# An S5 state-space block with a gated unit on one core: one full-row phase of TensorE per chunk, and a last output tile in parts of 192 and 256 columns

## The chip, the core and the metric

The kernel runs on one core of a Trainium2 chip. The metric is the device time of one execution in microseconds (us); lower is better. A profile comes with each run. Its span runs from the first to the last instruction of the core and is as a rule some 1.8 us shorter than the time measured from outside. All timed runs quoted here are fast ones (TensorE clock granted at 0.988 to 1.0), except one of a variant and two single runs, which are marked.

## The reference

2048 tokens of width D = 448 are normalised. One branch is a complex diagonal recurrence with 448 states and a skip term; the other is a gated unit with F = 1792. The output combines them.

```python
def reference(x, Lambda_re, Lambda_im, B_re, B_im, C_re, C_im, log_dt, Dskip, w_gate, w_up, w_down):
    xn = layernorm(x)                                   # (2048, 448)
    # --- state-space branch
    Lam_bar = exp(exp(log_dt) * Lam)                    # complex, 448 states
    B_bar = ((Lam_bar - 1) / Lam)[:, None] * B
    Bu = xn @ B_bar.T                                   # complex
    h[t] = Lam_bar * h[t - 1] + Bu[t]                   # 2048 steps
    s = 2 * real(h @ C.T) + xn * Dskip                  # xn * Dskip is the skip term
    # --- gated branch
    g = silu((sigmoid(xn @ w_gate) * (xn @ w_up)) @ w_down)
    return x + s * g                                    # bf16
```

## The kernel before

The tokens are worked on in 4 chunks of 512 (4 tiles of 128 each). TensorE has these kinds of work, and how many rows of its array they use matters here:

- **gate and up products**: 14 per chunk, each of seven 64-row *pairs* (two matmuls of 512 columns at once on the two halves of the array). Each goes to one of three PSUM buffers `gu`. A gate product is emptied by ScalarE (tanh), an up product by VectorE, which multiplies it with the tanh.
- **B projection**: the input of the recurrence, in four column groups. 448 = 3 x 128 + 64 input rows, so each group has full-row matmuls ("fulls") and one half-row pair. ScalarE copies the result to `bus` in SBUF.
- **down product** of a tile: 14 full-row matmuls of 448 columns; ScalarE's silu puts it into one of five buffers `g_t`.
- **output tile** (`yout`): 7 full-row matmuls; VectorE adds the skip term `xd`, multiplies by `g_t` and adds x; then a store.

The two PSUM banks `acc` take the down products and the output tiles in turn. The recurrence itself (rotation, scan, rotation back) is VectorE's. A planner places the instructions of ScalarE, VectorE and GpSimd by estimated costs and deadlines; TensorE's order is as written.

```python
def gu_mm(c, k, m, a, lo, hi, first):              # one gate or up product: 7 pairs
    def f():
        for s in range(7):
            T.matmul(gu[a][:, 0, ts], lhsT=w_[0:H, s, ms], rhs=x[0:H, s, ts], start=(s == 0), stop=(s == 6))
            T.matmul(gu[a][:, 1, ts], lhsT=w_[H:P, (s + 1) % 7, ms], rhs=x[H:P, s, ts], ...)
    ...
def gu_evac(c, k, m, a):
    if k == "g": add("ACT", ..., A.activation(th, gu[a][:], ACT.Tanh, scale=0.5), ...)
    else:        add("DVE", ..., V.scalar_tensor_tensor(out=ho, in0=th, scalar=1.0, in1=gu[a][:], op0=ALU.add, op1=ALU.mult), ...)

def b_units(c, pts, mid=None):                     # two column groups of the B projection
    slots = [next_gu() for _ in pts]
    def pairs():
        for pt, a in zip(pts, slots):              # half rows first (start=True)
            ...
    add("PE", 0.216 * len(pts), pairs, ...)
    if mid:
        mid()                                      # down products, in the same full-row stretch
    for n, (pt, a) in enumerate(zip(pts, slots)):
        def fulls(pt=pt, a=a):
            ...                                    # 2 x 3 matmuls, 512 columns (group 3: 256)
        add("PE", ..., fulls, ...)
        if pt < 3:
            add("ACT", act(1024), A.copy(out=bus[u][:], in_=gu[a][:]), ...)
        else:                                      # group 3: one copy of 512 columns, two of 64 rows
            add("ACT", act(512), ...); add("ACT", 0.6, ...); add("ACT", 0.6, ...)

def yout(c, j, first=False, banks=None, parts=((0, D),)):
    for pi, (c0, c1) in enumerate(parts):
        ...
        for i, (hm, cm) in enumerate(K_ORDER):     # 7 matmuls of c1 - c0 columns
            T.matmul(y, lhsT=hT[c % 2][:, hm, js], rhs=cT[:, cm, c0:c1], start=(i == 0), stop=(i == 6))
        V.tensor_tensor(out=od, in0=y, in1=xq[:, c0:c1], op=ALU.add)       # skip term
        V.tensor_tensor(out=od, in0=od, in1=g_t[g][:, c0:c1], op=ALU.mult)
        V.tensor_tensor(out=od, in0=od, in1=x_all[:, t, c0:c1], op=ALU.add)
        ...                                                                # store

# --- order of work (cut)
b_units(0, (0, 1)); b_units(0, (2, 3))             # chunk 0
...
for c in (2, 3):                                   # chunk 1 is alike
    for i in range(0, 4): gu_step(c, i)
    b_units(c, (0, 1), lambda: down(c - 1, 0, True))
    yout(c - 2, 0); down(c - 1, 1); yout(c - 2, 1)
    for i in range(4, 7): gu_step(c, i, i == 4)
    b_units(c, (2, 3), lambda: down(c - 1, 2, True))
    yout(c - 2, 2); down(c - 1, 3); yout(c - 2, 3)
    for i in range(7, 14): gu_step(c, i, i == 7)
    whole(c)                                       # the recurrence of chunk c
...
yout(3, 3, banks=[...], parts=((0, 128), (128, 448)))
```

## Time and profile before

| | before |
|---|---|
| time, median of 3 (range) | 186.65 us (186.59 to 187.62) |
| span of the profiled run | 185.5 us |
| TensorE, VectorE, ScalarE busy | 97%, 89%, 50% |
| matmuls; ScalarE instructions | 1375; 140 |
| switches between half-row and full-row work after 29 us | 17 |

The prediction shows the main lines. Two more, from the page's groups of instructions of the kernel before (line, engine, operation, output from input, shapes, count; busy us and mean ns; idle time before them and what ended most of it):

```profile
L709 PE MATMUL gu<-xnT,wU 64*128 64x512 bf16 x196 | 46.0, 376 | 0.0
...
L726 DVE SCALAR_TENSOR_TENSOR hF<-sig,gu 128x1024 bf16<-128x1024 f32 x21 | 25.4, 1212 | 1.9 <-PE gu L710 1.6
```

A pair shows 376 ns because its end is modelled; pairs start every 0.216 us. VectorE's evacuation of an up product lasts 1.21 us and in 21 of them it waited 1.9 us in all: VectorE rarely has time to wait for TensorE.

One line of the start, from the timeline of VectorE of the kernel before (start, duration, instruction, idle time and releaser in brackets), becomes important later. It is the first use of the x rows of chunk 1, which a transfer of 448 KB brings:

```profile
17.63 0.63 DVE L425 BATCH_NORM_STATS2 bst<-x_all 128x6 f32<-128x448 bf16 x1 [5.26 <-DMA x_all<-in_A_x_dram]
```

VectorE stood idle for 5.26 us until those rows landed, and everything that follows on VectorE starts from there.

### The profile page before, as it was taken

To read this page: it belongs to the slowest core of one execution; us is meant where nothing else is said; L and a number is where in the kernel's file an instruction comes from. 1 tells how busy PE (TensorE), PEld (TensorE's weight loads), DVE (VectorE), ACT (ScalarE), POOL (GpSimd) and SP (SyncE) were. 2 spreads that over 40 slices of the span, in tenths; PEclk is the share of its full clock that TensorE was granted. 3 is DMA by queue.
4 is the path that set the end of the run, shared out by engine and by line. 5 is a ranking of instruction groups with operands and counts; after the bars stand their busy time and mean duration, and the time that the engine had idled before them with its cause. 6 is when DMAs were issued, how large, how long until landed. Compare 5 with 4: busy or idle time off the path is not lost.

```text
span 185.5 us, 3527 instructions
## 1 busy us (share of the span) xinstructions
PE 179.9 (97%) x1375; PEld 88.5 (48%) x1375; DVE 165.8 (89%) x295; ACT 93.1 (50%) x140; POOL 38.5 (21%) x93
## 2 busy tenths in 40 slices
PE   7999999999999999999999999999999999999991
PEld 2675444464445444444445444444445544455550
DVE  3731999999989899999999999899999999999763
ACT  3449995973899994225375422427223516211110
POOL 7125451940168937000012100000000000000000
PEclk9999999999999999999999999999999999999998
DMA  5999999499302330000023300000000000002120
GB/s 159 257 221 225 176 175 210 80 269 178 120 4 46 82 71 4 0 0 4 0 51 78 73 26 0 4 25 24 0 25 4 25 25 4 25 0 76 51 78 25
DMA packets 30257, 13.43 MB, mean 72 GB/s; under 512 B 19744, under 2 KB 30240, under 8 KB 30240
## 3 DMA queue, kind: packets, MB, share of 16 engines
q1 hardware_dynamic: 28336, 12.05, 31.1%
q10 hardware_dynamic: 1808, 1.15, 2.5%
q8 instruction: 11, 0.18, 0.4%
q14 instruction: 6, 0.05, 0.1%
q0 software_dynamic: 96, 0.00, 0.0%
HBM read 6.77 MB, written 1.84 MB: 46 GB/s over the span
## 4 chain that ended last, share of the span: by engine, by line
PE 68%; DVE 15%; DMA 8%; ACT 4%; issue 2%; SPq 1%; DVEq 0%
PE gu L709 29%; PE acc L892 15%; PE acc L917 11%; PE gu L892 6%; DMA x_all<-in_A_x_dram 5%; PE gu L777 5%; DVE hF L726 4%; DMA wG<-in_B_w_gate_dram 3%; DVE wv L831 2%; DVE hT L581 1%; DVE bst L425 1%; ACT ctmp L675 1%; DVE ta L824 1%; PE gu L780 1%; DVE tb L825 1%
## 5 line engine op out<-in xcount | busy, mean ns | idle before, releaser
L709 PE MATMUL gu<-xnT,wG 64*128 64x512 bf16 (+1 forms) x231 | 46.1, 344 | 0.3 <-DVE xnT L510 0.3
L710 PE MATMUL gu<-xnT,wG 64*128 64x512 bf16 (+1 forms) x231 | 46.1, 344 | 0.0
L709 PE MATMUL gu<-xnT,wU 64*128 64x512 bf16 x196 | 46.0, 376 | 0.0
L710 PE MATMUL gu<-xnT,wU 64*128 64x512 bf16 x196 | 46.0, 376 | 0.0
L723 ACT ACTIVATE sig<-gu 128x1024 f32<-128x1024 f32 x21 | 21.4, 1022 | 30.3 <-PE gu L710 27.9
L892 PE MATMUL acc<-wd,hF 128*128 128x448 bf16 x168 | 33.8, 353 | 0.0
L892 PEld LDWEIGHTS <-hF 128*128 128x128 bf16 x224 | 21.4, 98 | 21.1 <-issue 1.7
L709 PEld LDWEIGHTS <-wG 64*128 64x128 bf16 x231 | 21.3, 94 | 20.9 <-issue 1.9
L709 PEld LDWEIGHTS <-wU 64*128 64x128 bf16 x196 | 18.1, 94 | 23.4 <-issue 1.3
L726 DVE SCALAR_TENSOR_TENSOR hF<-sig,gu 128x1024 bf16<-128x1024 f32 x21 | 25.4, 1212 | 1.9 <-PE gu L710 1.6
L831 DVE TENSOR_TENSOR_SCAN wv<-c_r,st,z 128x512 bf16<-128x512 f32 x18 | 22.9, 1275 | 0.0
L917 PE MATMUL acc<-cT,hT 128*128 128x448 bf16 (+1 forms) x112 | 22.4, 344 | 0.0
L710 PEld LDWEIGHTS <-wG 64*128 64x128 bf16 x231 | 21.2, 94 | 0.0
L710 PEld LDWEIGHTS <-wU 64*128 64x128 bf16 x196 | 18.1, 94 | 0.0
L777 PE MATMUL gu<-xnT,bT 128*128 128x512 bf16 x72 | 16.9, 379 | 0.0
L917 PEld LDWEIGHTS <-hT 128*128 128x128 bf16 x119 | 11.3, 98 | 10.0 <-issue 0.4
L898 ACT ACTIVATE g_t<-acc 128x448 bf16<-128x448 f32 x12 | 6.5, 540 | 16.1 <-PE acc L892 13.0
L425 DVE BATCH_NORM_STATS2 bst<-x_all 128x6 f32<-128x448 bf16 x12 | 7.0, 612 | 7.4 <-DMA x_all<-in_A_x_dram 7.4
L788 ACT CAST bus<-gu 128x1024 bf16<-128x1024 f32 x12 | 12.0, 1005 | 2.3 <-PE gu L777 2.3
L478 POOL COPY xn<-xn 128x64 bf16<-128x64 bf16 x12 | 5.9, 488 | 29.1 <-ACT xn L475 28.8
L923 DVE TENSOR_TENSOR o_t<-acc,xd 128x448 bf16<-128x448 f32 (+1 forms) x16 | 9.5, 595 | 2.6 <-PE acc L917 2.4
L898 ACT ACTIVATE g_t<-gu 128x448 bf16<-128x448 f32 x4 | 2.2, 544 | 18.8 <-PE gu L892 18.8
(142 smaller groups left out, 261.8 us busy)
## 6 DMA issues: line engine op xcount, KB each, us to landing
out_dram<-o_t SPq DMA_DIRECT2D x15, 112.0 KB, 1.7
wd<-in_B_w_down_dram SPq DMA_DIRECT2D x2, 784.0 KB, 5.1
x_all<-in_A_x_dram SPq DMA_DIRECT2D x3, 448.0 KB, 4.7
wU<-in_B_w_up_dram SPq DMA_DIRECT2D x2, 448.0 KB, 11.5
wU<-in_B_w_up_dram SPq DMA_DIRECT2D x2, 336.0 KB, 7.3
wG<-in_B_w_gate_dram SPq DMA_DIRECT2D x2, 224.0 KB, 6.1
wG<-in_B_w_gate_dram ACTq DMA_DIRECT2D x2, 224.0 KB, 6.2
xnT<-xn SPq DMA_TRANSPOSE x24, 2.4
```

What stands on the lines that cost most here:

```text
L425: add("DVE", 0.6, lambda: V.bn_stats(out=bst[b][:], in_=x_all[:, t, :]), r=[("x", t)], w=[("bst", b)])
L709: T.matmul(gu[a][:, 0, ts], lhsT=w_[0:H, s, ms], rhs=x[0:H, s, ts], start=(s == 0), stop=(s == 6))
L710: T.matmul(gu[a][:, 1, ts], lhsT=w_[H:P, (s + 1) % 7, ms], rhs=x[H:P, s, ts], start=(s == 0), stop=(s == 6))
L723: add("ACT", act(1024), lambda: A.activation(th, gu[a][:], ACT.Tanh, scale=0.5), r=[("gu", a)], w=[tk])
L726: add("DVE", dve1(1024), lambda: V.scalar_tensor_tensor(out=ho, in0=th, scalar=1.0, in1=gu[a][:], op0=ALU.add, op1=ALU.mult), r=[("gu", a) ...
L777: T.matmul(gu[a][:, i, :], lhsT=bT[:, kt, i, pt * P:pt * P + P], rhs=x[:, 2 * kt, :], start=False, stop=(kt == 2))
L788: add("ACT", act(1024), lambda u=u, a=a: A.copy(out=bus[u][:], in_=gu[a][:]), r=[("gu", a)], w=[("bus", u)])
L831: dve(1.194, lambda k=k: V.tensor_tensor_scan(out=wv[:, k, :], data0=rb, data1=z[:, k, :], initial=(st[pt][:, k, :] if c else 0.0), op0=AL ...
L892: T.matmul(d, lhsT=hF[c % 2][:, m, h, js], rhs=wd[:, ft, :], start=(ft == 0), stop=(ft == FT - 1))
L898: add("ACT", act(448), lambda: A.activation(g_t[g][:], d, ACT.Silu, scale=0.5), r=[key, "silutab"], w=[("gt", g)])
L917: T.matmul(y, lhsT=hT[c % 2][:, hm, js], rhs=cT[:, cm, c0:c1], start=(i == 0), stop=(i == 6))
L923: add("DVE", dve1(n), lambda od=od, y=y, c0=c0, c1=c1: V.tensor_tensor(out=od, in0=y, in1=xq[:, c0:c1], op=ALU.add), r=[key, ("xd", q)], w ...
```

## The change

The intent is to change less often between half-row and full-row work on TensorE, and to shorten VectorE's last instructions after the last matmul. The two `b_units` of a chunk become one `b_phase`: half rows of groups 3, 0 and 1; then their fulls; then all down products and output tiles; then the fulls of group 2, whose half rows come last, so that they join the half-row stream after it. Group 3 moves from a `gu` buffer to the two `acc` banks, with six evacuations of 256 columns. The last tile is cut at column 192, and the skip term of its second part is added by a matmul with the identity.

```diff
-    def b_units(c, pts, mid=None):
+    def b_phase(c, mid=None):
+        slots = [next_gu() for _ in range(3)]
+        a3 = (next_acc(), next_acc())
 ...
+                for h, (d, q, l) in enumerate(((slice(0, P), slice(0, P), 0), (slice(0, H), slice(H, P), 1),
+                                               (slice(H, P), slice(0, H), 1))):
+                    add("ACT", 0.3, lambda ...: A.copy(out=bus[u][d, l, ns], in_=acc[a3[i]][q, 0:256]), ...)
 ...
+        add("PE", 0.54, pairs, ...)                       # half rows of 3, 0, 1
+        for pt in (3, 0, 1):
+            add("PE", ..., lambda pt=pt: fulls(pt, False), ...)
+            evac(pt)
+        if mid:
+            mid()
+        add("PE", 1.29, lambda: fulls(2, True), ...)
+        add("PE", 0.22 + SW, lambda: halfrows(2, False), ...)
+        evac(2)
@@ yout
+            on_pe = len(parts) > 1 and pi == len(parts) - 1
+                if on_pe:
+                    T.matmul(y, lhsT=ident[:, :], rhs=xq[:, c0:c1], start=True, stop=False)
 ...
+            if on_pe:
+                V.tensor_tensor(out=od, in0=y, in1=g_t[g][:, c0:c1], op=ALU.mult)   # no add of xq
@@ order of work
-    b_units(0, (0, 1))
-    b_units(0, (2, 3))
-    for i in range(13, 14):
-        gu_step(0, i, i == 13)
+    gu_step(0, 13)
+    b_phase(0)
 ...
     for c in (2, 3):
+        def mid(c=c):
+            for j in range(4):
+                down(c - 1, j)
+                yout(c - 2, j)
         for i in range(0, 4):
             gu_step(c, i)
-        b_units(c, (0, 1), lambda: down(c - 1, 0, True))
-        ...                                               # yout, down, yout, three gu_steps
-        b_units(c, (2, 3), lambda: down(c - 1, 2, True))
-        ...
-        for i in range(7, 14):
-            gu_step(c, i, i == 7)
+        b_phase(c, mid)
+        for i in range(4, 14):
+            gu_step(c, i)
 ...
-    yout(3, 3, banks=[(("acc", a), acc[a]), free_banks[4]], parts=((0, 128), (128, 448)))
+    yout(3, 3, banks=[(("acc", a), acc[a]), free_banks[4]], parts=((0, 192), (192, 448)))
```

More of the change, by code (lines that the diff above doesn't have):

```diff
@@ L750 @@
     bus_n = [0]
-    def b_units(c, pts, mid=None):
+    def b_phase(c, mid=None):
         x = xnT[c % 3]
-        slots = [next_gu() for _ in pts]
-        bk = [("bT", 0), ("bT", 1), ("bT3", 0), ("bT3", 1), "bT3l"] + (
-            [("bT6", 0), ("bT6", 1)] + [("bT6", i, h) for i in range(2) for h in range(2)] if 3 in pts else [])
-        def pairs():
-            for pt, a in zip(pts, slots):
-                if pt < 3:
-                    ps = slice(pt * P, pt * P + P)
-                    T.matmul(gu[a][:, 0, :], lhsT=bT[0:H, 3, 0, ps], rhs=x[0:H, 6, :], start=True, stop=False)
-                    T.matmul(gu[a][:, 1, :], lhsT=bT[H:P, 3, 1, ps], rhs=x[H:P, 5, :], start=True, stop=False)
-                else:
-                    T.matmul(gu[a][:, 0, 0:256], lhsT=bT6[0:H, 3, :], rhs=x[0:H, 6, 0:256],
-                             start=True, stop=False)
-                    T.matmul(gu[a][:, 1, 0:256], lhsT=bT6[H:P, 3, :], rhs=x[H:P, 5, 256:512],
-                             start=True, stop=False)
-        add("PE", 0.216 * len(pts), pairs, r=xr(c) + bk, w=[("gu", a) for a in slots], name=f"bp{c}.{pts[0]}")
-        if mid:
-            mid()
-        for n, (pt, a) in enumerate(zip(pts, slots)):
-            def fulls(pt=pt, a=a):
-                for i in range(2):
-                    for kt in range(3):
-                        if pt < 3:
-                            T.matmul(gu[a][:, i, :], lhsT=bT[:, kt, i, pt * P:pt * P + P], rhs=x[:, 2 * kt, :],
-                                     start=False, stop=(kt == 2))
-                        else:
-                            T.matmul(gu[a][:, i, 0:256], lhsT=bT6[:, kt, :],
-                                     rhs=x[:, 2 * kt, i * 256:i * 256 + 256], start=False, stop=(kt == 2))
-            add("PE", (6 * 0.215 if pt < 3 else 6 * 0.11) + (0 if n or mid else SW), fulls,
-                r=xr(c) + bk + [("gu", a)], w=[("gu", a)], name=f"b{c}.{pt}")
@@ new lines, in b_phase, with halfrows @@
+        slots = [next_gu() for _ in range(3)]
+        a3 = (next_acc(), next_acc())
+        bk = [("bT", 0), ("bT", 1), ("bT3", 0), ("bT3", 1), "bT3l"]
+        bk6 = [("bT6", 0), ("bT6", 1)] + [("bT6", i, h) for i in range(2) for h in range(2)]
+        rs = [(slice(0, H), 6), (slice(H, P), 5)]
+        def halfrows(pt, start):
+            for i, (hs, s_) in enumerate(rs):
+                if pt < 3:
+                    T.matmul(gu[slots[pt]][:, i, :], lhsT=bT[hs, 3, i, pt * P:pt * P + P], rhs=x[hs, s_, :],
+                             start=start, stop=not start)
+                else:
+                    T.matmul(acc[a3[i]][:, 0:256], lhsT=bT6[hs, 3, :], rhs=x[hs, s_, i * 256:i * 256 + 256],
+                             start=start, stop=not start)
@@ new lines, in pairs, with fulls @@
+        def pairs():
+            for pt in (3, 0, 1):
+                halfrows(pt, True)
+        def fulls(pt, first):
+            for i in range(2):
+                for kt in range(3):
+                    if pt < 3:
+                        T.matmul(gu[slots[pt]][:, i, :], lhsT=bT[:, kt, i, pt * P:pt * P + P], rhs=x[:, 2 * kt, :],
+                                 start=(first and kt == 0), stop=(not first and kt == 2))
+                    else:
+                        T.matmul(acc[a3[i]][:, 0:256], lhsT=bT6[:, kt, :],
+                                 rhs=x[:, 2 * kt, i * 256:i * 256 + 256], start=False, stop=(kt == 2))
@@ L784, in b_units, with key, evac @@
+        def key(pt):
+            return [("gu", slots[pt])] if pt < 3 else [("acc", a) for a in a3]
+        def evac(pt):
             u = bus_n[0] % NBUS
@@ L787, in b_units @@
             if pt < 3:
-                add("ACT", act(1024), lambda u=u, a=a: A.copy(out=bus[u][:], in_=gu[a][:]),
-                    r=[("gu", a)], w=[("bus", u)])
-            else:
-                h2 = lambda t: t.rearrange("p (i n) -> p i n", i=2)
-                add("ACT", act(512), lambda u=u, a=a: A.copy(out=h2(bus[u][:, 0, :]), in_=gu[a][:, :, 0:256]),
-                    r=[("gu", a)], w=[("bus", u)])
-                add("ACT", 0.6, lambda u=u, a=a: A.copy(out=h2(bus[u][0:H, 1, :]), in_=gu[a][H:P, :, 0:256]),
-                    r=[("gu", a)], w=[("bus", u, 1)])
-                add("ACT", 0.6, lambda u=u, a=a: A.copy(out=h2(bus[u][H:P, 1, :]), in_=gu[a][0:H, :, 0:256]),
-                    r=[("gu", a)], w=[("bus", u, 2)])
+                add("ACT", act(1024), lambda: A.copy(out=bus[u][:], in_=gu[slots[pt]][:]), r=key(pt), w=[("bus", u)])
+                return
+            for i in range(2):
+                ns = slice(i * 256, i * 256 + 256)
+                for h, (d, q, l) in enumerate(((slice(0, P), slice(0, P), 0), (slice(0, H), slice(H, P), 1),
+                                               (slice(H, P), slice(0, H), 1))):
+                    add("ACT", 0.3, lambda ns=ns, d=d, q=q, l=l, i=i: A.copy(out=bus[u][d, l, ns], in_=acc[a3[i]][q, 0:256]),
+                        r=[("acc", a3[i])] + ([("bus", u, i, 0)] if h else []),
+                        w=[("bus", u) if h == i == 0 else ("bus", u, i, h)])
+        add("PE", 0.54, pairs, r=xr(c) + bk + bk6, w=key(3) + key(0) + key(1), name=f"bp{c}")
+        for pt in (3, 0, 1):
+            add("PE", (1.29 if pt < 3 else 0.66) + (SW if pt == 3 else 0), lambda pt=pt: fulls(pt, False),
+                r=xr(c) + bk + bk6 + key(pt), w=key(pt), name=f"b{c}.{pt}")
+            evac(pt)
+        if mid:
+            mid()
+        add("PE", 1.29, lambda: fulls(2, True), r=xr(c) + bk, w=key(2), name=f"b{c}.2")
+        add("PE", 0.22 + SW, lambda: halfrows(2, False), r=xr(c) + bk + key(2), w=key(2), name=f"bp{c}.2")
+        evac(2)
     bus_of = {}
@@ L858, in ssm_stack @@
         dve(dve2(1024), lambda: V.tensor_tensor(out=ta[:], in0=bus[u][:], in1=cs3[:], op=ALU.mult),
-            [("bus", u), ("bus", u, 1), ("bus", u, 2)] + tk, [("ta", ia)])
+            [("bus", u)] + [("bus", u, i, h) for i in range(2) for h in range(3) if i or h] + tk, [("ta", ia)])
         dve(dve2(512), lambda: V.tensor_tensor(out=z[:, 0, :], in0=ta[:, 0, :], in1=ta[:, 1, :], op=ALU.add),
@@ L913, in yout, with f @@
             y = y[:, 0:c1 - c0]
-            def f(y=y, c0=c0, c1=c1):
+            on_pe = len(parts) > 1 and pi == len(parts) - 1
+            def f(y=y, c0=c0, c1=c1, on_pe=on_pe):
+                if on_pe:
+                    T.matmul(y, lhsT=ident[:, :], rhs=xq[:, c0:c1], start=True, stop=False)
                 for i, (hm, cm) in enumerate(K_ORDER):
-                    T.matmul(y, lhsT=hT[c % 2][:, hm, js], rhs=cT[:, cm, c0:c1], start=(i == 0), stop=(i == 6))
+                    T.matmul(y, lhsT=hT[c % 2][:, hm, js], rhs=cT[:, cm, c0:c1],
+                             start=(i == 0 and not on_pe), stop=(i == 6))
             n = c1 - c0
-            add("PE", 7 * (0.004 + n / 2400.0) + (SW if first else 0), f,
-                r=cTk + [("hT", c % 2, p) for p in range(4)], w=[key], name=f"y{c}.{j}")
+            add("PE", (8 if on_pe else 7) * (0.004 + n / 2400.0) + (SW if first else 0), f,
+                r=cTk + [("hT", c % 2, p) for p in range(4)] + ([("xd", q), "ident"] if on_pe else []),
+                w=[key], name=f"y{c}.{j}")
             ok = ("o", o, pi)
             od = o_t[o][:, c0:c1]
-            add("DVE", dve1(n), lambda od=od, y=y, c0=c0, c1=c1: V.tensor_tensor(out=od, in0=y, in1=xq[:, c0:c1], op=ALU.add),
-                r=[key, ("xd", q)], w=[ok])
-            add("DVE", dve2(n), lambda od=od, c0=c0, c1=c1: V.tensor_tensor(out=od, in0=od, in1=g_t[g][:, c0:c1], op=ALU.mult),
-                r=[ok, ("gt", g)], w=[ok])
+            if on_pe:
+                add("DVE", dve1(n), lambda od=od, y=y, c0=c0, c1=c1: V.tensor_tensor(out=od, in0=y, in1=g_t[g][:, c0:c1], op=ALU.mult),
+                    r=[key, ("gt", g)], w=[ok])
+            else:
+                add("DVE", dve1(n), lambda od=od, y=y, c0=c0, c1=c1: V.tensor_tensor(out=od, in0=y, in1=xq[:, c0:c1], op=ALU.add),
+                    r=[key, ("xd", q)], w=[ok])
+                add("DVE", dve2(n), lambda od=od, c0=c0, c1=c1: V.tensor_tensor(out=od, in0=od, in1=g_t[g][:, c0:c1], op=ALU.mult),
+                    r=[ok, ("gt", g)], w=[ok])
             add("DVE", dve2(n), lambda od=od, c0=c0, c1=c1: V.tensor_tensor(out=od, in0=od, in1=x_all[:, t, c0:c1], op=ALU.add),
@@ L1005 @@
     prepare(2)
-    b_units(1, (0, 1), lambda: down(0, 0, True))
-    down(0, 1)
-    for i in range(3, 6):
-        gu_step(1, i, i == 3)
-    b_units(1, (2, 3), lambda: down(0, 2, True))
-    down(0, 3)
-    for i in range(6, 14):
-        gu_step(1, i, i == 6)
+    b_phase(1, lambda: [down(0, j) for j in range(4)])
+    for i in range(3, 14):
+        gu_step(1, i)
     whole(1)
     for c in (2, 3):
+        def mid(c=c):
+            for j in range(4):
+                down(c - 1, j)
+                yout(c - 2, j)
         for i in range(0, 4):
             gu_step(c, i)
-        b_units(c, (0, 1), lambda: down(c - 1, 0, True))
-        yout(c - 2, 0)
-        down(c - 1, 1)
-        yout(c - 2, 1)
-        for i in range(4, 7):
-            gu_step(c, i, i == 4)
-        b_units(c, (2, 3), lambda: down(c - 1, 2, True))
-        yout(c - 2, 2)
-        down(c - 1, 3)
-        yout(c - 2, 3)
+        b_phase(c, mid)
         if c == 2:
             prepare(3)
-        for i in range(7, 14):
-            gu_step(c, i, i == 7)
+        for i in range(4, 14):
+            gu_step(c, i)
         whole(c)
```

## The prediction

> **What bounds the kernel now.** I read the busy shares first, then the waits of TensorE, then the chain of work that ended last, then the timelines of TensorE and VectorE. First the busy line of the page, then the whole answer on TensorE's waits (engine, what it waited for: us, times, longest):
>
> ```profile
> PE 179.9 (97%) x1375; PEld 88.5 (48%) x1375; DVE 165.8 (89%) x295; ACT 93.1 (50%) x140; POOL 38.5 (21%) x93
> ...
> PE gu L419 <- DVE hF L378: 1.2, 1, 1.2
> PE gu L709 <- DVE xnT L510: 0.3, 1, 0.3
> ```
>
> TensorE hardly waits after the first microseconds, so what moves the time is its own instruction stream and the tail behind its last matmul. VectorE at 89% is a second limit close behind: between 80 and 107 us it is busy for 26.93 of 27.00 us (table by stretches).
>
> Two of TensorE's gaps are not waits. The stream alternates between 64-row matmuls, which run in pairs on the two halves of the array, and full 128-row ones. From the chain (start, us, what):
>
> ```profile
> 81.13 2.75 PE acc L892 x14
> 83.88 2.59 PE gu L777 x12
> 86.47 1.32 PE acc L917 x7
> 87.80 2.65 PE acc L892 x14
> 90.45 1.32 PE acc L917 x7
> 91.77 0.32 PE gu L709
> ```
>
> The same fourteen matmuls take 2.75 us when they follow half-row work and 2.65 when they follow full-row work. The first half-row pair after full-row work takes 0.32 where a pair otherwise takes 0.21 or 0.22. So **one switch, in either direction, costs 0.10 to 0.11 us**. Taking start to start over the whole trace I get 0.106 (0.096 before the switch, 0.010 at the slot after it), nearly the same for all.
>
> **What the Trainium skill says.** "TensorEngine Tiling (Array Packing)", section Key Properties: changing the tiling mode, not just the tile, drains the engine. The trace agrees and gives the size, 0.106 us. "TensorE: Matmul & The Clock Gate", section Back-to-back issue gap: N/2.4 + 2.5 ns when warm, which is 0.216 us for 512 columns and 0.189 for 448; the trace has 0.216 and 2.65/14 = 0.189. "VectorE: DVE Perf Modes", the tier table: tensor_tensor with bf16 in SBUF runs at 2x, with any PSUM operand at 1x; the trace has 0.39 us against 0.62 for 448 columns. "Perfetto Trace Analysis", section on the Tensor Engine instruction: VectorE and ScalarE are strict FIFOs. That matters below, because the change reorders VectorE.
>
> **The change part by part.**
>
> 1. *Switches.* From 29 us on the old stream has two full-row stretches in each of four chunks, which is sixteen switches, and one into the final output phase: 17. The new one has one stretch per chunk; its last half-row matmuls (for column group 2) come after the full ones, so they join the half-row stream that follows. That is 8 + 1 = 9. Saved: 8 x 0.106 = **0.85 us**, all on TensorE, so all on the path.
>
> 2. *One small stall.* The fourth column group used to take a gu buffer. In chunk 1 it waited there for a ScalarE tanh (timeline of TensorE):
>
> ```profile
> 54.36 0.38 PE L762 MATMUL gu<-xnT,bT 64*128 64x512 bf16 x1
> 54.36 0.38 PE L763 MATMUL gu<-xnT,bT 64*128 64x512 bf16 x1
> 54.82 0.27 PE L765 MATMUL gu<-xnT,bT 64*128 64x256 bf16 x1
> ```
>
> The gap is 0.46 instead of 0.21. The group now goes to the two acc banks, which are long free there. Saved: **0.25 us**.
>
> 3. *Six evacuations instead of three for that group.* The old ones (128x512, 64x512, 64x512) take 0.59 us each. The 1024-column copy takes 1.00, so the slope is 0.41 / 512 = 0.8 ns a column and 256 columns are about 0.38 (an estimate). Six make 2.3 us against 1.8. ScalarE is at 50%, and the next user of the first acc bank comes two groups (2 x 1.29 us) later: hidden.
>
> 4. *A reordering that the diff doesn't show.* The scheduler places everything anew. The program order of VectorE, new against old, moves one L579 and two L581 (the sine tables) ahead of the first evacuation of chunk 0's "up" products. Old timeline of VectorE:
>
> ```profile
> 22.43 0.18 DVE L459 RECIPROCAL rsd<-sdb 128x4 f32<-128x4 bf16 x1
> 22.64 0.16 DVE L460 SCALAR_TENSOR_TENSOR nmr<-mv,rsd 128x4 f32<-128x4 bf16 x1
> 22.82 2.35 DVE L726 SCALAR_TENSOR_TENSOR hF<-hF,gu 128x1024 bf16<-128x1024 bf16 x2
> ...
> 26.64 0.45 DVE L579 TENSOR_SCALAR hT<-hT 128x513 f32<-128x513 f32 x1
> 27.02 2.39 DVE L726 SCALAR_TENSOR_TENSOR hF<-hF,gu 128x1024 bf16<-128x1024 bf16 x2
> 29.32 1.29 DVE L581 SCALAR_TENSOR_TENSOR hT<-hT,hT 128x513 f32<-128x513 f32 x2
> ```
>
> From start to start L579 costs 0.36 and two L581 cost 1.21. Nothing that they need is late, so the first L726 starts at 22.82 + 1.57 = 24.39 and ends 1.21 later, at 25.60. The gu ring has three buffers, so the fourth "up" product needs this very buffer, and the old trace starts that product at 24.96. With 0.06 for the signal TensorE waits until about 25.66: **0.70 us lost** on a stream that was dense there. The evacuations that follow come every 1.14 us against 1.51 of matmuls for each, so the loss doesn't grow.
>
> 5. *Last tile.* Old timeline of VectorE:
>
> ```profile
> 180.58 0.29 DVE L923 TENSOR_TENSOR o_t<-acc,xd 128x128 bf16<-128x128 f32 x1 [1.22 <-PE acc L917]
> 180.97 0.23 DVE L925 TENSOR_TENSOR o_t<-o_t,g_t 128x128 bf16<-128x128 bf16 x1
> 181.24 0.23 DVE L927 TENSOR_TENSOR o_t<-o_t,x_all 128x128 bf16<-128x128 bf16 x1
> 181.53 0.49 DVE L923 TENSOR_TENSOR o_t<-gu,xd 128x320 bf16<-128x320 f32 x1
> 182.06 0.33 DVE L925 TENSOR_TENSOR o_t<-o_t,g_t 128x320 bf16<-128x320 bf16 x1
> 182.41 0.32 DVE L927 TENSOR_TENSOR o_t<-o_t,x_all 128x320 bf16<-128x320 bf16 x1
> ```
>
> On TensorE the first part grows from 7 x 0.056 to 7 x 0.0825 = 0.58 us, so its sum is ready 0.19 later, at 180.77 on the old clock. Sized between the rows of 128 and 320 columns its three steps are about 0.46 + 0.30 + 0.30, until 181.83. The second part's eight matmuls of 0.109 would be ready at 181.64, so it now waits for VectorE; then 0.46 for 256 columns from PSUM and 0.30 for the last add give 182.59. The old end is 182.73. Saved: **0.15 us**; the instruction dropped is worth more, but the larger first part eats most of it.
>
> Sum: -0.85 - 0.25 + 0.70 - 0.15 = -0.55, and 186.65 - 0.55 = **186.1 us**.
>
> **Rivals.**
>
> *A: no new stall at 25 us.* If the L579 and L581 find a gap, or the fourth product is later than I think, the 0.70 doesn't appear and the time is 185.4. Against it: the order is fixed in the program, and the old trace has no idle VectorE between 20 and 24 us.
>
> *B: VectorE becomes the bound.* With four down products and four output tiles in a row, the evacuations crowd into other places. I laid the old durations along the new order by hand. The "up" evacuations start 0.3 to 1.2 us after they are ready, and each has about 1.7 us until its buffer is needed. The tightest place is the second output tile in the last long stretch: its VectorE add ends about 0.5 us before the acc bank is needed again. The last state product would be done 2.0 us before its output tile (3.8 us in the old trace: 169.78 against 173.6). So I expect no stall, but a VectorE that falls behind by a microsecond would stall TensorE there. Two or three such places would cost 0.5 to 1.5 us: 186.6 to 187.6.
>
> *C: the silu of a down product comes late.* ScalarE now has eleven instructions between the tanh work and the first silu in chunk 3, two of them waiting for a VectorE scan. By hand it ends just as the second down product wants the bank. A stall of 0.1 to 0.5 us is possible: 186.2 to 186.6.
>
> **Range and chances.** The sure part is the switches (0.85). The spread is the new stall (0 to 0.9) and rivals B and C (0 to 1.0), and the old kernel's own three times differ by 1.0. I take 185.3 to 187.0. Two per cent are 3.7 us; no part comes near that, so within 2% is nearly certain.
>
> **What would show it.** In the chain or the timeline of the new trace: two slots with 0.10 more per chunk, not four (step 1); no 0.46 gap at the half-row pair of the fourth group (step 2); a TensorE gap of about 0.7 us near 25 us, released by VectorE's L726 (step 4); the last part's first VectorE instruction following the first part's last add at once, and ending about 0.75 after its start (step 5). The prediction is wrong if TensorE's waits list anything over 0.3 us on an acc bank after 80 us (B, C), or nothing near 25 us (A).

## The result and the profile after

| | before | after |
|---|---|---|
| time in the same rounds, median of 6 (range) | 187.23 us (186.59 to 187.80) | 185.96 us (185.63 to 186.08) |
| span of the profiled run | 185.5 us | 183.9 us |
| mean granted clock | 0.997 | 0.999 |
| matmuls in the trace; weight loads; ScalarE instructions | 1375; 1375; 140 | 1369; 1376; 152 |

The ratio is 0.9931 (95% interval 0.9906 to 0.9957), so within 2%. A ratio here is the mean time of one kernel's fast runs over the mean of the other's in the same rounds, so it is not quite the ratio of the medians quoted. It corresponds to 1.3 us. The run-to-run spread of before was 1.2 us in the same rounds, which is why the rest of this document goes by the starts of instructions in the traces rather than by times. The smaller number of matmuls is not the change's doing: some records are missing from the traces (the repeat of the unchanged kernel before shows 1368), and the weight loads, one per matmul, show the one matmul that was added, with the identity.

First the busy line of the page and the whole answer on TensorE's waits of the kernel after:

```profile
PE 178.5 (97%) x1369; PEld 89.6 (49%) x1376; DVE 165.8 (90%) x294; ACT 94.8 (52%) x152; POOL 34.5 (19%) x93
...
PE gu L419 <- DVE hF L378: 1.2, 1, 1.2
PE gu L709 <- DVE xnT L510: 0.3, 1, 0.3
```

TensorE is still the bound, and the list of its waits is the same as before: the expected wait near 25 us isn't in it. Next the chain of work that ended last, kernel after (start, duration, what):

```profile
79.88 0.43 PE gu L763 x4
80.31 0.76 PE acc L780 x6
81.12 2.54 PE gu L777 x11
83.66 2.65 PE acc L905 x14
...
100.85 0.32 PE gu L763 x2
```

In this stretch there are two switches. One lies between the half-row work at 79.88 and the first full-row group; the other is the 0.32 at 100.85, a pair that otherwise takes 0.216. All down products (L905) now take 2.65, since none directly follows half-row work. (One of the twelve L777 at 81.12 has no record.) The new place of group 3 shows in the timeline of TensorE in chunk 1, kernel after:

```profile
40.84 0.27 PE L766 MATMUL acc<-xnT,bT 64*128 64x256 bf16 x2
40.95 0.59 PE L763 MATMUL gu<-xnT,bT 64*128 64x512 bf16 x4
```

The pair at 40.84 writes to the acc banks and the next starts 0.11 later, with no gap like the 0.46 of before. The six evacuations are one line in the timeline of ScalarE, kernel after:

```profile
42.02 2.28 ACT L797 CAST bus<-acc 128x256 bf16<-128x256 f32 x6 [1.30 <-PE acc L780]
```

They take 2.28 us, as estimated (2.3), and nothing waits for them. Now the start, timeline of VectorE, kernel after:

```profile
16.80 0.63 DVE L425 BATCH_NORM_STATS2 bst<-x_all 128x6 f32<-128x448 bf16 x1 [4.72 <-DMA x_all<-in_A_x_dram]
...
21.90 0.42 DVE L579 TENSOR_SCALAR hT<-hT 128x513 f32<-128x513 f32 x1
22.23 1.29 DVE L581 SCALAR_TENSOR_TENSOR hT<-hT,hT 128x513 f32<-128x513 f32 x2
23.44 2.35 DVE L726 SCALAR_TENSOR_TENSOR hF<-hF,gu 128x1024 bf16<-128x1024 bf16 x2
```

The reordering is there as predicted: one L579 and two L581 now stand ahead of the first L726. But the x rows reached VectorE at 16.80 instead of 17.63, so the first L726 started at 23.44, not 24.39. TensorE shows what was left of the wait, timeline of TensorE, kernel after:

```profile
24.45 0.38 PE L709 MATMUL gu<-xnT,wU 64*128 64x512 bf16 x1
...
24.71 0.37 PE L709 MATMUL gu<-xnT,wU 64*128 64x512 bf16 x1
```

The distance is 0.254 where 0.216 is dense: a gap of 0.04 us. Last, the tail, timeline of VectorE, kernel after:

```profile
179.51 0.36 DVE L946 TENSOR_TENSOR o_t<-acc,xd 128x192 bf16<-128x192 f32 x1 [0.99 <-PE acc L934]
...
180.27 0.26 DVE L950 TENSOR_TENSOR o_t<-o_t,x_all 128x192 bf16<-128x192 bf16 x1
180.44 0.42 DVE L943 TENSOR_TENSOR o_t<-gu,g_t 128x256 bf16<-128x256 f32 x1
180.90 0.29 DVE L950 TENSOR_TENSOR o_t<-o_t,x_all 128x256 bf16<-128x256 bf16 x1
```

The second part's first instruction follows the first part's last by 0.17 us. Together, from the starts of instructions in the two traces:

| section | before | after | difference | what it is made of |
|---|---|---|---|---|
| start to first up product | 20.43 | 20.14 | -0.29 | differs from run to run (19.8 to 20.4 over the nine traces with the transfers in their original order, in both kernels) |
| first up product to chunk 1 | 16.30 | 16.14 | -0.16 | two switches -0.21, gap at 24.7 us +0.04, rest |
| chunk 1 to the last down product | 140.61 | 139.81 | -0.80 | six switches -0.64, stall at group 3 -0.25, a new stall of 0.10 |
| last down product to the end of VectorE | 5.40 | 5.10 | -0.30 | the last tile |

The three sections that the change touches give -1.26 us. The new stall of 0.10 lies at 165.5 us: a down product waits for a PSUM bank, whose silu on ScalarE waits for a `g_t` buffer. The timeline of ScalarE, kernel after, names it:

```profile
164.90 0.54 ACT L911 ACTIVATE g_t<-gu 128x448 bf16<-128x448 f32 x1 [6.46 <-DVE o_t L948]
```

Its releaser is the VectorE multiplication (L948) that reads the oldest of the five g_t buffers. A sixth buffer should take it away, but it doesn't fit into SBUF beside the rest, so this is not shown and its cost is read from the trace alone.

### The profile page after: what moved, and what is told of

The parts are those of the page before. It is cut to its first block, busy times and chain, and to the rows that moved or that the text cites. A ratio compares the mean times of both kernels' runs of the same rounds, so it can differ in the third digit from the quotient of the medians.

```text
span 183.9 us, 3540 instructions
## 1 busy us (share of the span) xinstructions
PE 178.5 (97%) x1369; PEld 89.6 (49%) x1376; DVE 165.8 (90%) x294; ACT 94.8 (52%) x152; POOL 34.5 (19%) x93
## 3 DMA queue, kind: packets, MB, share of 16 engines
q10 hardware_dynamic: 1808, 1.15, 2.4%
## 4 chain that ended last, share of the span: by engine, by line
PE 96%; DVE 1%; issue 0%; DVEq 0%
PE gu L709 45%; PE acc L905 17%; PE acc L934 11%; PE gu L777 8%; PE gu L905 6%; PE gu L419 2%; PE acc L780 2%; PE gu L763 2%; PE gu L710 1%; PE acc L502 1%; PE acc L503 0%; DVE xnT L510 0%; DVE o_t L950 0%; PE acc L766 0%; DVE o_t L946 0%
## 5 line engine op out<-in xcount | busy, mean ns | idle before, releaser
L905 PE MATMUL acc<-wd,hF 128*128 128x448 bf16 x168 | 33.2, 352 | 0.0
L905 PEld LDWEIGHTS <-hF 128*128 128x128 bf16 x224 | 21.9, 98 | 20.7 <-issue 0.2
L709 PEld LDWEIGHTS <-wG 64*128 64x128 bf16 x231 | 21.5, 94 | 20.2 <-issue 0.7
L709 PEld LDWEIGHTS <-wU 64*128 64x128 bf16 x196 | 18.4, 94 | 22.3
L726 DVE SCALAR_TENSOR_TENSOR hF<-sig,gu 128x1024 bf16<-128x1024 f32 x21 | 25.6, 1217 | 2.4 <-PE gu L710 1.8
L710 PEld LDWEIGHTS <-wG 64*128 64x128 bf16 x231 | 21.5, 94 | 0.0
L710 PEld LDWEIGHTS <-wU 64*128 64x128 bf16 x196 | 18.3, 94 | 0.2 <-issue 0.2
L777 PE MATMUL gu<-xnT,bT 128*128 128x512 bf16 x65 | 15.3, 379 | 0.4
L797 ACT CAST bus<-acc 64x256 bf16<-64x256 f32 (+1 forms) x24 | 8.7, 369 | 5.1 <-PE acc L780 4.9
L905 PE MATMUL gu<-wd,hF 128*128 128x448 bf16 x56 | 11.2, 352 | 0.0
```

The costliest lines, as they stand in the source:

```text
L726: add("DVE", dve1(1024), lambda: V.scalar_tensor_tensor(out=ho, in0=th, scalar=1.0, in1=gu[a][:], op0=ALU.add, op1=ALU.mult), r=[("gu", a) ...
L777: T.matmul(gu[slots[pt]][:, i, :], lhsT=bT[:, kt, i, pt * P:pt * P + P], rhs=x[:, 2 * kt, :], start=(first and kt == 0), stop=(not first a ...
L797: add("ACT", 0.3, lambda ns=ns, d=d, q=q, l=l, i=i: A.copy(out=bus[u][d, l, ns], in_=acc[a3[i]][q, 0:256]), r=[("acc", a3[i])] + ([("bus", ...
L905: T.matmul(d, lhsT=hF[c % 2][:, m, h, js], rhs=wd[:, ft, :], start=(ft == 0), stop=(ft == FT - 1))
```

## The experiments

**The theory** after the result: the change is worth 1.26 us by the sum in the table, and a wait at the fourth up product comes and goes with the moment at which the x rows of chunk 1 land. In the new order that product can't start earlier than 7.91 us after the landing (24.71 - 16.80). In the old order VectorE reaches its evacuation 1.45 earlier (5.19 instead of 6.64 after the landing), so the limit there is 7.91 - 1.45 = 6.46. TensorE's own turn for this product comes 4.53 us after the first up product (21 pairs of 0.2159). So the gap should be

landing + 7.91 - (first up product + 4.53), if positive.

**The rival**: the wait near 25 us doesn't exist in the new order (rival A of the prediction), and the difference between runs has another source.

### The two halves of the change alone

The first kernel has the new phases with the old last tile, the second the reverse.

```diff
 # phase_only: the kernel after, but with the yout of before and
+    parts=((0, 128), (128, 448))
 # tail_only: the kernel before, but with the yout of after and
+    parts=((0, 192), (192, 448))
```

> The new full-row phases with the old last tile (128 and 320 columns, both sums on VectorE). Theory A (the gain of 1.27 us is eight switches at 0.106, the 0.25 us stall of chunk 1 and about 0.29 us of tail): this kernel is 0.85 + 0.25 = 1.1 us faster than before, less 0.1 for small stalls, so 0.9 to 1.1 us (ratio 0.994 to 0.995), and its tail from the first matmul of the last down product to the last VectorE instruction is again 5.39 us as in the trace before. Rival B (the phases bring less because part of the gain seen was an earlier start or the tail): under 0.6 us faster. TensorE waits near 25 us only if the x rows of chunk 1 land later than 17.3 us.

> The old phases with the new last tile (192 and 256 columns, skip term of the last part on TensorE). The prediction: 0.15 us faster. Theory A: about 0.3 us faster, as the two traces show 5.39 us before and 5.10 after from the first matmul of the last down product to the last VectorE instruction. Rival B (the tail carries most of the 1.27 us): over 0.6 us. Rival C (the end is hidden behind the last store anyway): 0.0.

Phases alone: median 186.16 us (186.09 to 188.04), ratio 0.9969 (0.9923 to 1.0015), against 187.14 for before. Tail alone: 186.90 (186.50 to 187.58), ratio 0.9986 (0.9949 to 1.0023). Neither interval excludes 1, but the traces are plain. Phases alone took the long middle section from 140.61 to 139.81 and left the tail at 5.40; tail alone took the tail to 5.10 and left the middle at 140.84 (with the stall at group 3 at 0.47 this time). So in the traces the halves add up, and no part of the gain comes from their meeting. The medians (-0.98 and -0.24, sum -1.22) fit this but are too noisy to show it: two of the six runs of phases alone took 187.54 and 188.04, so its ratio, which goes by means, misses the expected 0.994 to 0.995. One more expectation failed: TensorE waited 0.42 us near 25 us with the x rows at 16.84, not only after 17.3. By the formula above the limit is 16.41 in this run (its first up product came at 19.79).

### Both kernels again, and the x transfer moved

The x rows of chunk 1 are the third of five transfers that one queue issues: two halves of the first up weights, x, two halves of the second. The variants change only the order in which these five are issued, after the plan is made, so the order of every compute engine stays as it was.

```diff
+    five_ = pl.ops[n0_:n0_ + 5]
+    fns_ = [five_[i].fn for i in (2, 0, 1, 3, 4)]      # xfirst;  xlate: (0, 1, 3, 4, 2)
+    for o_, f_ in zip(five_, fns_):
+        o_.fn = f_
```

> The changed kernel unaltered, for a second trace and the spread of the start. If the landing of the x rows of chunk 1 (17.6 us in the trace before, 16.8 in the one after) varies from run to run, this trace shows another value between 16 and 18.5, and the TensorE gap at the fourth up product follows it one to one above about 16.8: landing at 17.6 would give a gap of 0.5 us or more there. If the new order of instructions itself brought the rows earlier, it is 16.8 again and the gap is 0.04. Time against before: ratio 0.993.

> The kernel before, unaltered, against itself: ratio 1.000 within 0.2 per cent. A second trace: the 0.25 us stall at the fourth group of chunk 1 appears again if it belongs to the program; the x rows of chunk 1 land at 17.6 us again if that belongs to the program, at another time if it is by chance.

> The changed kernel with one transfer moved: the x rows of chunk 1 are issued ahead of the first two up-weight blocks instead of after them; the order on every compute engine is unaltered. Theory (the gap at the fourth up product is the x landing + 7.91 us less the product's turn at about 24.7): the rows land before 14 us, so the gap is gone in every run, the stretch from the first up product to chunk 1 is 16.1 us, and the slow ones among the changed kernel's times (186.8 and 187.0) do not come back: median 185.4 to 185.9 and ratio 0.991 to 0.994 to before. Rival (those slow times come from something else, or the up weights now come late): spread as before, or TensorE waits for the up weights near 20 us.

> The changed kernel with the x rows of chunk 1 issued after all up-weight blocks; the order on every compute engine is unaltered. Theory: the rows land near 20 us, so the gap at the fourth up product is about 20 + 7.9 - 24.8 = 3.1 us (in the trace: landing + 7.91 less the product's turn, to 0.1 us), and the kernel is 2 to 3 us slower than the changed one. Rival (VectorE isn't what the product waits for): gap under 0.5 us.

> The kernel before with the same early x rows. Theory: its order of instructions puts the evacuations ahead of the last sine tables, so it had no gap at the fourth up product in any of the traces, and the early rows give nothing: ratio 0.998 to 1.002, the stretch from the first up product to chunk 1 stays 16.30 us. Rival (the early rows speed up the start in both kernels): ratio under 0.997.

> The kernel before with the late x rows. Theory: here the first evacuation starts 5.19 us after the landing instead of 6.64, so the gap at the fourth up product is landing + 6.46 less about 24.9: 1.5 us for a landing at 20, some 1.5 us less than in the changed kernel with the same landing. Rival (the reordering costs nothing): the same gap in both.

The repeat of the kernel before had its x rows at 17.24, no wait at the fourth up product, and the stall at group 3 again (0.25). The repeat of the unchanged kernel after happened to show the wait. Timelines of VectorE (first fence) and TensorE (second) of that run:

```profile
18.14 0.63 DVE L425 BATCH_NORM_STATS2 bst<-x_all 128x6 f32<-128x448 bf16 x1 [5.84 <-DMA x_all<-in_A_x_dram]
...
24.78 1.22 DVE L726 SCALAR_TENSOR_TENSOR hF<-hF,gu 128x1024 bf16<-128x1024 bf16 x1
```

```profile
26.05 0.37 PE L709 MATMUL gu<-xnT,wU 64*128 64x512 bf16 x1 [0.99 <-DVE hF L726]
```

Here the same kernel waited 0.99 us for L726 (a distance of 1.37 instead of 0.216, so a gap of 1.15). The rows had landed at 18.14, 1.34 later than in the first run. The waits of TensorE of the two late variants, the kernel after first, the kernel before second (the line numbers are two higher there):

```profile
PE gu L711 <- DVE hF L728: 3.2, 1, 3.2
```

```profile
PE gu L711 <- DVE hF L728: 1.9, 1, 1.9
...
PE gu L764 <- DVE hF L728: 0.4, 1, 0.4
```

The gaps beside the formula, which was made from the first run of after:

| run | x rows on VectorE | first up product | gap by the formula | gap in the trace |
|---|---|---|---|---|
| after | 16.80 | 20.14 | (made from it) | 0.04 |
| phases alone | 16.84 | 19.79 | 0.43 | 0.42 |
| after again | 18.14 | 20.36 | 1.16 | 1.15 |
| after, x first | 13.09 | 19.88 | none | none |
| after, x late | 20.06 | 20.03 | 3.41 | 3.40 |
| after, cut at 128 (below) | 16.57 | 19.87 | 0.08 | 0.08 |
| after, skip term on VectorE (below) | 16.62 | 19.82 | 0.18 | 0.17 |
| before | 17.63 | 20.43 | none (with 6.46 for 7.91) | none |
| before, x late | 20.24 | 20.13 | 2.04 (with 6.46) | 2.04, and 0.54 later |

Where the formula gives a gap, the six rows that it wasn't made from agree to 0.01 us, so rival A falls: the wait is real, and how long it is depends on the landing and on the start of the first up product. The late variants show that the new order makes it longer: 3.40 against 2.04 for nearly the same landing. In the sections between the first up product and chunk 1 they lost 3.36 (after) and 2.59 (before). The expected gaps (3.1 and 1.5) were made with guessed moments; with those of the traces the formula holds.

The times, against 187.17 for before (187.14 for the first two rows, which ran earlier):

| kernel | median (range), us | ratio (interval) |
|---|---|---|
| after again | 185.84 (185.38 to 187.03) | 0.9936 (0.9894 to 0.9977) |
| before again | 187.26 (186.65 to 188.83) | 1.0017 (0.9970 to 1.0065) |
| after, x first | 185.74 (185.40 to 187.38) | 0.9936 (0.9890 to 0.9982) |
| after, x late | 188.96 (188.88 to 190.48; 3 runs, a slow fourth of 192.36 left out) | 1.0129 (1.0059 to 1.0199) |
| before, x first | 187.43 (186.86 to 188.37) | 1.0010 (0.9970 to 1.0049) |
| before, x late | 190.04 (189.82 to 191.40; 4 runs) | 1.0163 (1.0114 to 1.0213) |

The profiled run of after again, with the gap of 1.15, has a span of 185.3 us; the shortest span of the same kernel in the same rounds is 183.6. What the x transfer first doesn't do is remove all long times: one of six still took 187.38, against the expectation. The gap can't be the cause if the rows landed as in the profiled run (13.09); only one run of each kernel has a trace, so this stays open. Before with x first gained nothing. Its order has no gap to remove, and in the profiled run TensorE waited 1.2 us for gate weights and reached the first up product at 21.22.

### More switches

Two gate/up products were put inside the full-row stretch of chunks 1 to 3, which adds twelve switches and no other work.

```diff
+    def mid1():
+        for j in range(4):
+            down(0, j)
+            if j in (0, 2):
+                gu_step(1, 3 + j // 2)
+    b_phase(1, mid1)
+    for i in range(5, 14):
-    b_phase(1, lambda: [down(0, j) for j in range(4)])
-    for i in range(3, 14):
 ...                                    # chunks 2 and 3 alike
```

> The changed kernel with switches put back: in chunks 1, 2 and 3 two gate or up products of the chunk are moved into the long full-row phase as half-row islands, so 12 switches more and no work more. Theory (each switch costs 0.106 us on the path): the stretch from chunk 1 to the last down product grows from 139.81 to 141.08 us (+1.27), each switch in the trace 0.10 to 0.11, and the kernel loses most of its gain, ratio to before 0.998 to 1.001. Rival (the gain of the long phases comes from how the buffers are used, not from the switches): the stretch grows by under 0.5 us.

It took 194.23 us (193.98 to 196.22), ratio 1.0361 (1.0311 to 1.0412), and the middle section grew by 7.45 us, not by the 1.27 of twelve switches: the expectation failed. In the trace the switches without a wait cost the usual 0.096 + 0.010 (a few cost 0.02 more). The rest is in the waits of TensorE (first fence) and in its timeline at the first of the long waits (second), same run:

```profile
PE gu L709 <- ACT bus L791: 5.7, 4, 2.6
```

```profile
49.45 0.37 PE L709 MATMUL gu<-xnT,wU 64*128 64x512 bf16 x1 [0.90 <-ACT bus L791]
```

The two products inside took two turns of the ring of three buffers. So in chunk 1 the first of them (49.45), and in each chunk the first product after the phase, needed a `gu` buffer that ScalarE had not yet copied to `bus`. Taken start to start, the added waits sum to 6.26 us, and 6.26 + 1.27 - 0.10 (the stall at 165.5, gone here) = 7.43. So the trace bears out the price of a switch, while the time of this kernel measures something else: how much the phase leans on free `gu` buffers around it. A kernel that differs in switches alone was not run; their price rests on the starts of instructions in the traces.

### The last tile, one factor at a time

The kernel after, with either the old cut or the old skip term, completes a square with the tails already measured.

```diff
 # tail_128_pe
-    parts=((0, 192), (192, 448))
+    parts=((0, 128), (128, 448))
 # tail_192_dve
-            on_pe = len(parts) > 1 and pi == len(parts) - 1
+            on_pe = False
```

> The changed kernel with the last tile cut at 128 instead of 192 columns, skip term of the last part still on TensorE; judged by the trace, first matmul of the last down product to the end of the last VectorE instruction (5.40 us in the old kernel, 5.10 in the changed one). Worked out from the durations: the second part is ready 1.68 us after the tile's first matmul and needs 0.49 + 0.04 + 0.32, so 5.17. The skip term on TensorE then gives 0.23 and the new cut 0.07. Rival (the cut is what counts): 5.35 or more.

> The changed kernel cut at 192 columns, but with the skip term of both parts on VectorE as in the old kernel; judged by the trace. Worked out: VectorE is busy with the first part until 1.71 us after the tile's first matmul, then 0.46 + 0.33 + 0.29, so 5.44, no gain over 5.40. Rival (the cut is what counts): 5.15 or less.

From the first matmul of the last down product to the end of VectorE, us:

| | skip term on VectorE | skip term on TensorE |
|---|---|---|
| cut at 128 | 5.40 | 5.18 |
| cut at 192 | 5.43 | 5.10 |

Both came out as expected (5.17 and 5.44). The identity matmul is worth 0.22 us with the old cut. The new cut is worth 0.08, but only together with the matmul; by itself it costs 0.03. With the cut at 128, VectorE is done early with the first part and waits for the second part's sum; at 192 it goes on at once. The second part's first instruction with the cut at 128 and the identity matmul (first fence), and with the cut at 192 and the skip term on VectorE, after the first part's last add (second fence), from the timelines of VectorE:

```profile
180.18 0.49 DVE L943 TENSOR_TENSOR o_t<-gu,g_t 128x320 bf16<-128x320 f32 x1 [0.21 <-PE gu L934]
```

```profile
180.08 0.26 DVE L950 TENSOR_TENSOR o_t<-o_t,x_all 128x192 bf16<-128x192 bf16 x1
180.26 0.42 DVE L946 TENSOR_TENSOR o_t<-gu,xd 128x256 bf16<-128x256 f32 x1
```

(One run each, 185.61 and 185.95 us, state not known; the times don't resolve this, the traces do.)

### A version from these findings

The x transfer is issued first, the last tile is cut at 256, and both parts' skip terms are added by TensorE.

```diff
+    fns_ = [five_[i].fn for i in (2, 0, 1, 3, 4)]
-            on_pe = len(parts) > 1 and pi == len(parts) - 1
+            on_pe = len(parts) > 1
-    parts=((0, 192), (192, 448))
+    parts=((0, 256), (256, 448))
```

> The changed kernel with the early x rows of chunk 1 and a last tile of 256 and 192 columns with the skip term of both parts on TensorE. Theory: no gap at the fourth up product, and a tail of about 5.05 us instead of 5.10; the median 185.3 to 185.8 us, ratio to before 0.989 to 0.994, so the best of all by a hair that the times may not resolve. Rival: the earlier rows delay another load, the ratio is no better than 0.994.

It took 185.58 us (185.29 to 186.07), ratio 0.9880 (0.9840 to 0.9921) to before (187.89 in this call). The tail was 5.09, hardly below 5.10 and short of the 5.05 expected. There was no gap at the fourth up product (rows at 13.82). It beats the kernel before. Whether it beats the kernel after isn't resolved: 185.58 against 185.84 and 185.96. They were run at other times.

## Why the prediction was right, and where it wasn't

The time of 186.1 us was off by 0.14 us from the measured 185.96, and the change is within 2% as forecast. Part of that closeness is luck. The kernel before ran at 187.23 in these rounds instead of 186.65, and the predicted saving of 0.55 was too small by 0.7; the two errors nearly cancel.

1. **Switches: right.** 17 became 9, those without a wait cost 0.106 in every trace (a few up to 0.02 more), and eight fewer are -0.85 (-0.21 in chunk 0, -0.64 later).
2. **The small stall at the fourth group: right.** It is gone in all eight traces with the new order of work (the variant with more switches not counted). In the old ones it was 0.25 to 0.53, so 0.25 is the low end of what it costs.
3. **Six evacuations: right.** 2.28 us per chunk, hidden.
4. **The reordering on VectorE: mechanism right, term mis-sized.** The prediction took 0.70. The step that failed is "the first L726 starts at 22.82 + 1.57 = 24.39", because 22.82 belongs to one run's landing of the x rows (17.63). In the profiled run the rows landed 0.83 earlier, and the term was 0.04: 0.70, less 0.83, plus 0.29 because the first up product came 0.29 earlier too, less 0.12 because the moved instructions cost 1.45 and not 1.57. In the four other traces of this order with the transfers unmoved it was 0.08 to 1.15, so it is a quantity with a spread and not a number. "Nothing near 25 us" was named as what would prove the prediction wrong, and the first trace's waits indeed list nothing there; that one trace would have led to the wrong conclusion, that the wait doesn't exist. The repeat shows it.
5. **Last tile: direction right, term mis-sized.** -0.30 instead of -0.15. The prediction let 0.30 us pass between the start of the first part's last add and the start of the second part's multiplication. That is the distance of two instructions of which the second needs the result of the first (179.97 to 180.27). These two are independent and are 0.17 apart, which gives 0.13 of the missing 0.15. TensorE did not set this distance: it is 0.18 in the kernel with the skip term on VectorE (180.08 to 180.26), where the sum was ready earlier.

Of the rivals, A is right for the first run's outcome but wrong in its reason: neither a gap for the sine-table instructions nor a later fourth product made room, but an early transfer. B did not come: VectorE is busy for 90% of the span, and no wait for an acc bank after 80 us shows in the waits of any new trace of the same phases. C came in another place than expected and small: 0.10 us at 165.5. With the measured terms the prediction's sum is -0.85 - 0.25 + 0.04 - 0.30 + 0.10 = -1.26, which is what the sections show.

## What to carry to other kernels

On a kernel bound by TensorE, count how often the row mode of the array changes; the price of a change can be read from the trace (0.106 us here), and moving the half-row part of an accumulation to the end of its group can join it to the next half-row stretch. When a change reorders another engine, compare its order instruction by instruction, and express the new wait as a distance from the event that starts that engine's work, here a transfer; then look at that event in several runs before putting a number on the wait. A matmul with the identity in an accumulation that runs anyway takes an add off VectorE, and how a tail is best cut depends on which engine then ends last.

## What the Trainium skill lacked or had wrong

- "TensorEngine Tiling (Array Packing)", section Key Properties, says that a change of tiling mode drains TensorE, without a size. Here a change between 64-row pairs and full rows costs 0.106 us each way (0.096 before it, 0.010 at the slot after), in all traces, where nothing else is waited for.
- "TensorE: Matmul & The Clock Gate", section Back-to-back issue gap, says that a stream of weight loads and matmuls sustains about 131 ns per matmul of 512 columns and that N/2.4 + 2.5 over-counts there. Here such a stream (twelve L777 matmuls in 2.59 us in the kernel before) takes 0.216 us each, which is that formula; the measurement decides.
- "VectorE: DVE Perf Modes", section The DRAIN you can't avoid, says that the next instruction doesn't start until the pipe is empty, and adds that one that isn't held starts earlier, without a figure. Here an independent one started 0.17 us after an instruction of 0.26 us (180.27 and 180.44), and a dependent one 0.30 us after one of the same length (179.97 and 180.27).
- No page that I found gives the spread of a transfer's landing between executions. Here the same 448 KB, issued in the same order, reached VectorE between 16.57 and 18.14 us in nine traces; in the five of them with the new order on VectorE, TensorE's wait at the fourth up product was 0.04 to 1.15 us.
